# New instruction orders, earlier mask and x loads, and GpSimd splits from partition 0 in an LSH attention with a routed expert layer

## The chip, the cores and the metric

The kernel runs on one core of one Trainium2 chip, in one launch. The metric is the device time of that core in microseconds (us). Five engines work side by side, each through its own instruction queue in program order: TensorE (PE in the profile, its weight loads PEld), VectorE (DVE), ScalarE (ACT), GpSimd (POOL) and SyncE (SP, which here only issues DMAs).

## The reference

Inputs are q, k, v of shape (4, 8, 768, 64) in float32, a projection of 64x6, and the gate and two weight matrices of 8 experts (512x1024 and 1024x512). Attention is masked by hash buckets: a query sees only the keys whose six sign bits agree with its own. The output goes through an expert layer in which each token goes to one expert.

```python
q_bits = (np.einsum('bhsd,dk->bhsk', q, proj) > 0)      # likewise k_bits; bucket = the 6 bits as a number
mask = q_bucket[:, :, :, None] == k_bucket[:, :, None, :]
scores = np.where(mask, scale * np.matmul(q, k.transpose(0, 1, 3, 2)), -1e9)
attn = softmax(scores);  x = np.matmul(attn, v)          # rows of x: 3072 tokens x 512
expert_idx = np.argmax(x @ w_gate, axis=1)
y = np.maximum(x @ w1[e], 0.0) @ w2[e]                   # for the tokens of expert e
out = gate_w[:, None] * y
```

## The kernel before

**Pairs and passes.** The 32 heads are worked as 16 pairs (4 batches of 4 pairs). The loop at line 1076 makes one pass for each pair and runs through a written list of short tokens: HEAD in pass 0, PLAN in passes 1 to 14, LAST in pass 15. `step` (line 986) turns a token into instructions. A token with "-" behind it belongs to the pair before (one "-" for each pair back), so a pass g mixes the scores of pair g with the end of pairs g-1 and g-2 and the preparation of pair g+1. Every engine executes its share of the tokens in the order of the list. The lists are thus the order of the work on all queues.

**The tokens of a pass.** A pair has 12 score units (128 queries of one head by 768 keys).
- S: four matmuls of a unit (lines 291 and 293) into one of three PSUM tiles named s. R: VectorE takes the row's extreme and copies to SBUF (line 301), which frees the PSUM tile. X: ScalarE's exponential (line 307).
- The probabilities are then transposed, for one half of the units by TensorE (T, line 321, evacuated by E, lines 369 and 371, through two PSUM tiles named t), for the other half by VectorE in 32x32 blocks (D, line 343) into one SBUF tile `ZT`. Behind the sixth D of a pair, SyncE issues 16 DMAs (line 349) that carry the blocks to their places in `pt`. `ZT` has one buffer (the room named w2, and w0 for the last two pairs), so the first D of a pair waits until the 16 DMAs of the pair before have landed.
- V: probabilities times v (24 matmuls, line 381), O its evacuation (line 387). K and L: the rows of the pair with the gate's product (lines 401 and 411). M: the sums (line 391).
- I: SyncE's loads for pair g+2, `loads` (line 953): q and k of the pair for the hash (`load_pair`, line 82), q and k of each head (`load_x`, line 77, 768 KB each), v (`load_v`, line 87, which waits for the V of the pair before), and in the early passes the filling of the rows that no token takes (`fill`, line 148, 1.2 MB each, for the eight experts in turn).

**The preparation of the next pair.** A: ScalarE scales k (line 1039). P0 to P3 for one head and P4 to P7 for the other: GpSimd splits q and k into a high and a low part (`split`, lines 186 to 200) in a tile of four planes. Plane 2 and plane 3 get hash bits in 16 rows. G: TensorE's hash products (line 249), H: their signs on ScalarE (line 232), B: GpSimd weighs them and writes them to memory (lines 259 and 260). N: GpSimd issues two DMAs (line 264) that bring the bits into planes 2 and 3 of the two heads, once P1, P2, P5 and P6 are done and B's write has landed. In the code this is called a mask; the first S of the next pair waits for it.

**Routing.** When a batch of four pairs is done, its tokens are routed (`route`, line 421, a chain of small VectorE operations with a few matmuls in between, of which the tokens R and G of the next passes carry some steps each) and their rows are written to the expert's rows by GpSimd's indirect DMAs (`scatter`, line 475, in passes 7, 8, 11, 12, 14 and 15, one behind an R each). `route_step` (line 936) says behind which R of a pass: k counts the R tokens of the pass.

**The expert layer.** In LAST, GpSimd also prepares the first expert's weights (n and t, lines 898 and 904; `weights`, lines 655 and 656) in the rooms w0 to w3, and the first matmuls of the expert layer are put in (m, line 763). From then on the expert layer runs through all experts (lines 763, 800, 820).

**Last pair.** Its x is loaded at the start of pass 14 (line 1079), into the tiles named xd. The x of the other odd pairs goes into `room`, the room w3 (line 71).

## Time and profile before

| what | value |
|---|---|
| time, median of 3 runs (lowest to highest) | 754.92 us (747.46 to 757.76) |
| the profiled execution's own time | 753.52 us |
| its span in the profile | 751.7 us |
| TensorE busy | 707.0 us, 94% of the span |
| VectorE, ScalarE, GpSimd busy | 452.1, 428.3, 458.0 us |
| DMA, mean over the span | 195 GB/s |

The profile shows one execution. A row of its groups of instructions gives the line of the kernel, the engine, the operation, and out<-in by the names of the tiles; in a timeline, the start, the duration, the engine and line, and in brackets how long the engine had been idle before and what ended the wait. PEclk is the clock granted to TensorE, as a share of full speed. The pass borders used below are the starts of TensorE's first instruction of a pass.

### The profile page before, as it was taken

To read this page: it belongs to the slowest core of one execution; us is meant where nothing else is said; L and a number is where in the kernel's file an instruction comes from. 1 tells how busy PE (TensorE), PEld (TensorE's weight loads), DVE (VectorE), ACT (ScalarE), POOL (GpSimd) and SP (SyncE) were. 2 spreads that over 40 slices of the span, in tenths; PEclk is the share of its full clock that TensorE was granted. 3 is DMA by queue.
4 is the path that set the end of the run, shared out by engine and by line. 5 is a ranking of instruction groups with operands and counts; after the bars stand their busy time and mean duration, and the time that the engine had idled before them with its cause. 6 is when DMAs were issued, how large, how long until landed. Compare 5 with 4: busy or idle time off the path is not lost.

```text
span 751.7 us, 12370 instructions
## 1 busy us (share of the span) xinstructions
PE 707.0 (94%) x4219; PEld 578.0 (77%) x4219; DVE 452.1 (60%) x929; ACT 428.3 (57%) x864; POOL 458.0 (61%) x492
## 2 busy tenths in 40 slices
...
GB/s 314 214 265 229 279 265 308 295 150 283 294 206 242 231 243 276 241 271 150 171 228 174 117 96 83 254 152 169 170 130 164 142 132 185 191 131 189 125 10 38
DMA packets 68849, 146.69 MB, mean 195 GB/s; under 512 B 15811, under 2 KB 29507, under 8 KB 68720
## 3 DMA queue, kind: packets, MB, share of 16 engines
...
q10 hardware_dynamic: 144, 0.02, 0.0%
HBM read 89.35 MB, written 26.33 MB: 154 GB/s over the span
## 4 chain that ended last, share of the span: by engine, by line
PE 48%; DMA 13%; POOL 8%; issue 3%; DVE 2%; ACT 2%; SPq 1%; POOLq 0%; DVEq 0%; ACTq 0%
PE s L763 20%; PE s L800 10%; PE s L820 9%; DMA masks<-bits 4%; DMA w<-masks 3%; DMA sorted_rows<-xr,slot 2%; PE t L321 2%; PE t L381 2%; PE s L291 2%; PE s L293 2%; DMA qk<-masks 1%; SPq L349 1%; POOL w L197 1%; DMA sorted_rows<-sorted_rows 1%; POOL qk L197 1%
## 5 line engine op out<-in xcount | busy, mean ns | idle before, releaser
L301 DVE TENSOR_SCALAR_CACHE_REDUCE e<-s 128x768 f32<-128x768 f32 x192 | 178.8, 948 | 79.7 <-PE s L293 46.6
L307 ACT ACTIVATE e<-e,m 128x768 f32<-128x768 f32 x192 | 178.2, 931 | 10.6 <-DVE e L301 8.1
L659 POOL TENSOR_TENSOR w<-raw,w 128x512 fp32r<-128x512 f32 x112 | 144.8, 1316 | 36.2 <-ACT w L658 35.0
L381 PE MATMUL t<-pt,vt 128*64 128x384 f32 x768 | 129.5, 493 | 3.9 <-ACT pt L371 3.9
L763 PE MATMUL s<-xh,w 128*128 128x456 f32 (+6 forms) x672 | 126.8, 346 | 0.0
L371 ACT ACTIVATE pt<-t 128x512 f32<-128x512 f32 (+1 forms) x152 | 84.3, 584 | 72.1 <-PE t L321 69.6
L763 PEld LDWEIGHTS s<-xh,w 128*128 128x128 f32 x672 | 119.2, 188 | 3.1
L381 PEld LDWEIGHTS t<-pt,vt 128*64 128x64 f32 x768 | 54.2, 138 | 71.5 <-issue 64.2
L779 DVE SCALAR_TENSOR_TENSOR hh<-s,hh 128x256 fp32r<-128x256 f32 (+7 forms) x64 | 35.5, 555 | 107.1 <-ACT hh L777 100.3
L321 PE MATMUL t<-ident,e 128*128 128x128 f32 x648 | 95.3, 283 | 3.2 <-ACT e L307 2.1
L343 DVE STREAM_TRANSPOSE w<-e 128x768 f32<-128x768 f32 x84 | 77.5, 957 | 24.0 <-DMA pt<-w 13.9
L321 PEld LDWEIGHTS t<-ident,e 128*128 128x128 f32 x648 | 79.6, 146 | 12.7 <-ACT e L307 3.8
L777 ACT ACTIVATE hh<-s 128x256 fp32r<-128x256 f32 (+7 forms) x64 | 31.4, 490 | 90.8 <-PE s L763 90.8
L800 PE MATMUL s<-hh,w 128*128 128x456 f32 (+3 forms) x384 | 74.9, 355 | 0.0
L800 PEld LDWEIGHTS s<-hh,w 128*128 128x128 f32 x384 | 71.1, 188 | 2.7
L291 PE MATMUL s<-qk 80*128 80x384 f32 x192 | 57.6, 383 | 13.1 <-DMA qk<-masks 11.9
L291 PE MATMUL s<-w 80*128 80x384 f32 x192 | 56.2, 374 | 13.8 <-DMA w<-masks 13.8
L658 ACT ACTIVATE w<-raw 128x512 fp32r<-128x512 f32 x112 | 66.3, 622 | 0.6 <-DMA raw<-in_w1p_dram 0.6
...
L820 PE MATMUL s<-w,hh 128*128 128x512 f32 (+1 forms) x240 | 56.4, 394 | 0.0
L820 PEld LDWEIGHTS s<-w,hh 128*128 128x128 f32 (+1 forms) x240 | 44.6, 187 | 10.5
L293 PE MATMUL s<-qk 128*128 128x384 f32 x192 | 52.1, 355 | 0.0
...
## 6 DMA issues: line engine op xcount, KB each, us to landing
...
```

The lines of the kernel that those rows point to most:

```text
L291: nc.tensor.matmul(p[:, a, :HALF], k[0:80, 2, c], k[0:80, 3, n], start=i >= 4, stop=i < 4)
L293: nc.tensor.matmul(p[:, a, :HALF], k[:, 0, c], k[:, 1, n], start=i < 4, stop=i >= 4)
L301: nc.vector.tensor_scalar(e, SC.pop(i)[:, :, :HALF], CEIL, None, op0=OP.min, op1=OP.min, accum_out=m)
L307: nc.scalar.activation(e, e, AF.Exp, bias=m, scale=-1.0, accum_out=SM[g, hf][:, t, s:s + 1])
L321: nc.tensor.transpose(o[:, j, w], e[w][:, kt // 3, (kt % 3) * 128:(kt % 3) * 128 + 128], ident)
L343: nc.vector.transpose(z[:, :, c, w].rearrange("p g (k i) -> p g k i", i=32), e)
L371: nc.scalar.activation(o, x, AF.Copy)
L381: nc.tensor.matmul(p[s * 64:(s + 1) * 64, :HALF], VT[g][:, kt, s, :], PT[u][:, :, :, s, kt].rearrange("p a t i -> p t a i"), start=(kt == ...
L659: nc.gpsimd.tensor_tensor(w[:, 1, a], r, w[:, 0, a], op=OP.subtract)
L763: nc.tensor.matmul(p[:, :c], w[:, a, d, fs], x[:, b, d, :c], start=(k == 0), stop=(k == 11))
L800: nc.tensor.matmul(p[:, :c], w[:, a, f % 4, ms], h[b][:, f, :c], start=(k == 0), stop=(k == 23))
L820: nc.tensor.matmul(p[:pw], HH[n][b][:, f, i:i + pw], w[:, a, f % 4], start=(k == 0), stop=(k == 23))
```

## The change

- `split` k = 3 (P3, P7): the copy of q covers all 128 partitions, and the subtraction that makes the low part works on partitions 0 to 63 in place of 64 to 127 (it takes the high part from the tile's own plane 0 in place of plane 2). High and low halves of plane 0 change places; the product over both halves is the same sum.
- The last pair's x goes into `room` like that of other odd pairs and is loaded by token I of pass 13 in place of at the start of pass 14. Its split tiles move to the rooms w2 and w1, and the first expert's weight chunks to the rooms in the order of HOME.
- `fill` of experts 2 to 7: expert 2 in pass 0 behind token w, experts 3 to 7 in passes 1 to 5 (before: experts 2 to 7 in passes 1 to 6).
- `route_step`: the first seven steps of a batch's routing run behind R number 7 to 11 of the pass in portions of 2, 1, 2, 1 and 1 (before: one behind each of R number 2 to 8).
- New lists HEAD, PLAN and LAST with nearly the same tokens. In PLAN, G, H and B stand at the head of the pass, N stands ahead of V1 and V0 in place of behind them, the splits come in the order P5 P1 P0 P2 P4 P6 N P7 P3 (before P5 P7 P4 P6 P0 P1 P2 N P3).

```diff
@@ -72,7 +72,7 @@
 
     def load_x(h):
         g = h // 2
-        x = room[:, h % 2] if g % 2 and g < NG - 1 else wk.tile([128, 2 * S], F32, name="xd")
+        x = room[:, h % 2] if g % 2 else wk.tile([128, 2 * S], F32, name="xd")
         for c in ((S, 2 * S), (0, S)) if h < 2 else ((0, 2 * S),):
             nc.sync.dma_start(x[:, c[0]:c[1]], qk2[h][:, c[0]:c[1]])
         XD[h] = x
@@ -176,7 +176,7 @@
     def qk_tile(h):
         g = h // 2
         if g == NG - 1:
-            QK[h] = moe.tile([128, 4, S], F32R, name=f"w{2 + h % 2}")
+            QK[h] = moe.tile([128, 4, S], F32R, name=f"w{2 - h % 2}")
         elif g % 2 and g < NG - 1:
             QK[h] = moe.tile([128, 4, S], F32R, name=f"w{h % 2}")
         else:
@@ -196,8 +196,8 @@
         elif k == 2:
             nc.gpsimd.tensor_tensor(t[0:80, 3], x[0:80, S:], t[0:80, 1], op=OP.subtract)
         else:
-            nc.gpsimd.tensor_copy(t[0:64, 0], x[0:64, :S])
-            nc.gpsimd.tensor_tensor(t[64:128, 0], x[64:128, :S], t[64:128, 2], op=OP.subtract)
+            nc.gpsimd.tensor_copy(t[:, 0], x[:, :S])
+            nc.gpsimd.tensor_tensor(t[0:64, 0], x[0:64, :S], t[0:64, 0], op=OP.subtract)
 
     ENG = {"A": nc.scalar, "V": nc.vector, "P": nc.gpsimd}
 
@@ -626,6 +626,7 @@
 
 
     CH, RAW = {}, {}
+    HOME = "w0", "w3", "w2", "w1", "w4", "w5"
     P2 = {}
 
     def raw_load(c, a):
@@ -649,7 +650,7 @@
 
         if a == 0:
             s = c % 6
-            CH[c] = (moe if s < 4 else P2["p"]).tile([128, 2, 4, 512], F32R, name=f"w{s}")
+            CH[c] = (moe if s < 4 else P2["p"]).tile([128, 2, 4, 512], F32R, name=HOME[s])
         w, r = CH[c], RAW[c, a // 2][:, a % 2]
         if c < 4:
             nc.gpsimd.tensor_copy(w[:, 0, a], r)
@@ -890,7 +891,7 @@
             k = parts.pop(0)
             c, a = divmod(k, 4)
             if a == 0:
-                CH[c] = moe.tile([128, 2, 4, 512], F32R, name=f"w{c}")
+                CH[c] = moe.tile([128, 2, 4, 512], F32R, name=HOME[c])
             o, i = CH[c][:, 0, a], RAW[c, a // 2][:, a % 2]
             if x == "A":
                 nc.scalar.activation(o, i, AF.Copy)
@@ -909,26 +910,26 @@
     lows = []
 
     HEAD = """
-        k01A k00V j00V y01 q00A j01V p00A y00 l00V b03 b00 i02 f0 p01P b02 q01P b01 k11A i12 f1 k10A j11V y11 R0 j10V
-        l01P y10 q11P l11P q10A l10P S1 S8 p11P p10A b10 b13 b12 X0 s10 R1 X1 S2 G H w R8 X8 s12 R2 X2 S5 R5 X5 s01 S6
-        s00 S3 T01 s02 z0 S4 s11 z1 s13 b11 E01v s03 T00 E00a T02 R3 S7 E02v X3 T10 E10a R4 X4 T11 T12 E11v E12a R6 X6
-        R7 X7 T20 E20v S9 T21 E21v S10 T22 R9 E22a T30 E30a X9 T31 E31v T32 E32a R10 S11 R11 T41 E41a X10 T40 E40v T42
-        E42v
+        k01A k00V j00V y01 q00A j01V p00A y00 l00V b03 b00 i02 f0 p01P b02 q01P b01 k11A i12 f1 k10A j11V y11 R0 l01P
+        q10A p10A b13 y10 j10V b12 q11P b10 p11P S8 R8 S2 R2 G l10P S3 R3 l11P X0 H w S6 R6 S1 S4 X2 X3 T11 s11 s00
+        s01 s02 S5 b11 X6 X8 s10 s12 z1 z0 E11v s13 T10 E10v T12 R1 S9 X1 T01 R9 E12a E01v X9 T00 E00v S7 T02 E02a R7
+        R4 T41 E41a T40 T42 E40a E42v R5 S10 X7 T31 E31v T30 E30v S11 T32 E32v X4 X5 T20 E20a T21 M0 E21a T22 R11 X11
+        s03 E22v
     """.split()
 
     PLAN = """
-        K1-- R6- R10- X6- L0-- R11- T31- X10- E31a- X11- P5 S1 L1-- R1 S3 T30- E30a- T32- S5 E32a- T50- T51- R3 P7
-        E50a- S4 T52- E51a- R5 R4 S0 X3 S2 G A1 P4 E52a- S9 X4 X1 R2 H X5 S8 V1- M0- A0 X2 P6 B D3 O1- D1 R8 P0 D4 P1
-        V0- R0 R9 X8 X0 S7 X9 O0- D2 D0 T41 E41a I T40 S6 D5 S10 T42 P2 E40a R7 M1- X7 E42a N K0- P3 S11
+        R6- G L0-- X6- H P5 T30- S1 R11- T31- E30a- B R10- R1 K1-- X11- P1 S4 E31a- T32- L1-- S2 X10- M0- T50- R4
+        E32a- T51- E50a- S5 R2 M1- A0 T52- X4 E52a- P0 E51a- X2 A1 P2 P4 X1 R5 S3 S0 R3 S9 D4 S8 P6 X5 N V1- D2 X3 R9
+        O1- D5 V0- R0 R8 X9 D3 X0 S7 X8 I O0- T41 P7 E41a T40 D0 D1 R7 S6 T42 E40a S11 K0- E42a P3 X7 S10
     """.split()
 
     LAST = """
-        nP nP R6- X6- R10- X10- R11- T30- nP S3 tP L0-- E30v- S2 tP R2 X11- M1- T51- E51a- T50- E50a- X2 tP S0 T52-
-        E52a- R3 X3 R0 S7 K1-- L1-- S1 T31- E31v- X0 S5 T32- R1 E32a- X1 V1- O1- R5 X5 T01 E01v T00 E00a nP tP S4 T02
-        E02a T10 E10a R4 nP tP nP tP R7 S10 M0- T11 E11a nP tP X4 X7 S9 T12 R10 X10 E12v R9 X9 V0- O0- x2 g2 h2 S11
-        T20 E20a K0- L0- M0 nP tP S6 T21 E21a S8 T22 E22a R6 R11 X11 X6 V0 O0 T50 E50a T51 E51a T52 E52a R8 T30 E30a
-        T31 E31v T32 E32v X8 T40 E40a T41 E41a T42 E42a K0 L0 r0 r0 r0 M1 V1 r0 O1 K1 r0 r0 r0 L1 c0 K1- L1- r1 r1 r1
-        r1 r1 r1 r1 c1 x0 g0 h0 m6 u6 d6 m7 u7 d7 m4 u4 m3 u3 d4 d3 m2 u2 d2 m1 u1 d1 m0 u0 d0 m5 u5 d5
+        nP tP R6- X6- R11- L0-- K1-- L1-- R10- M0- X11- T31- M1-- E31a- T30- E30a- T32- S5 E32v- nP tP S4 X10- T50-
+        E50a- T51- E51a- R5 X5 R4 X4 S0 R0 X0 S3 T52- E52v- R3 X3 M1- S1 R1 X1 S6 V1- O1- T00 E00a S10 T20 E20a T21
+        E21v S2 T22 R2 R10 X10 E22v V0- O0- nP tP T01 T02 E01v E02v S8 X2 T11 E11a T10 E10a R6 X6 nP tP nP tP nP tP R8
+        X8 S11 K1- L1- M0 nP tP S9 K0- L0- S7 nP tP T12 E12a V0 R11 X11 R9 X9 O0 T41 E41a T40 T42 E40a E42a T51 E51a
+        R7 X7 K0 L0 r0 r0 T50 E50a T52 E52a T30 E30a r0 x0 T31 E31v T32 E32a x2 g2 r0 h2 M1 r0 r0 r0 c0 V1 O1 K1 L1 r1
+        r1 r1 r1 r1 r1 r1 c1 g0 h0 m2 u2 m3 u3 m4 d2 u4 m6 u6 d3 d4 d6 m7 u7 d7 m5 u5 d5 m0 u0 d0 m1 u1 d1
     """.split()
 
     SCAT = {}
@@ -936,10 +937,10 @@
     def route_step(g, k, since):
 
         b, q = divmod(g - NP, NP)
-        if 0 <= b < B - 1 and q == 1 and k == 2:
-            routes[b] = route(b, (0, 1))
-        if 0 <= b < B - 1 and q == 1 and k != "G" and 2 <= k <= 8:
-            go(routes[b], 1)
+        if 0 <= b < B - 1 and q == 1 and k != "G" and k >= 7:
+            if k == 7:
+                routes[b] = route(b, (0, 1))
+            go(routes[b], (2, 1, 2, 1, 1)[k - 7])
         if 0 <= b < B - 1 and q == 2:
             go(routes[b], 2 if k == "G" else 1 if since in (1, 2) else 0)
         if g in (7, 8, 11, 12) and k in (2, 5, 8) or g == 14 and since in (3, 4, 5) or g == 15 and k in (0, 1, 2):
@@ -954,7 +955,7 @@
 
         if g + 2 < NG:
             load_pair(g + 2)
-        if g + 2 < NG - 1:
+        if g + 2 < NG:
             load_x(2 * g + 4)
             load_x(2 * g + 5)
         if g + 1 < NG:
@@ -965,7 +966,7 @@
         g, r = divmod(c, 6)
         if 0 < g < NG - 1:
             return
-        if g + 2 < NG and r in (0, 2) and g + 2 != NG - 1:
+        if g + 2 < NG and r in (0, 2):
             load_x(2 * g + 4 + r // 2)
         if g + 1 < NG and r == 4:
             load_v(g + 1)
@@ -1008,8 +1009,8 @@
             trans(6 * n + int(x[0]), int(x[1]))
         elif op == "I":
             loads(n)
-            if 0 < n < 7:
-                fill(n + 1)
+            if 0 < n < 6:
+                fill(n + 2)
         elif op == "D" and n:
             blocks(12 * n + int(x))
         elif op == "E":
@@ -1075,9 +1076,6 @@
     last = [route(B - 1, (0,)), route(B - 1, (1,))]
     for g in range(NG):
         peaks, since = 0, 0
-        if g == NG - 2:
-            load_x(2 * g + 2)
-            load_x(2 * g + 3)
         for w in HEAD if g == 0 else LAST if g == NG - 1 else PLAN:
             if w == "G":
                 route_step(g, w, 0)
@@ -1085,6 +1083,8 @@
             step(g, w)
             if g == 0 and w in ("z0", "z1"):
                 fill(int(w[1]))
+            if g == 0 and w == "w":
+                fill(2)
             if w[0] == "R":
                 route_step(g, peaks, since)
                 if g == NG - 2 and 0 < since < 5:
```

## Rows read from the trace of the kernel before

**Rows 1.** The page's first part: busy time, share of the span, instructions.
```profile
PE 707.0 (94%) x4219; PEld 578.0 (77%) x4219; DVE 452.1 (60%) x929; ACT 428.3 (57%) x864; POOL 458.0 (61%) x492
```

**Rows 2.** Stretches: length, busy and (instructions) of PE PEld DVE ACT POOL, PEclk, DMA, GB/s.
```profile
52.20:79.40 27.20, 24.84 (x154) 18.66 (x154) 18.33 (x37) 18.97 (x39) 15.25 (x16) 0.94 0.85 248
...
104.10:127.10 23.00, 23.00 (x154) 17.15 (x153) 17.34 (x37) 18.70 (x39) 14.47 (x15) 1.00 0.95 295
...
150.50:182.30 31.80, 26.19 (x162) 19.97 (x161) 20.68 (x45) 19.39 (x39) 14.78 (x17) 0.89 0.68 205
...
356.60:386.10 29.50, 25.10 (x160) 17.76 (x159) 20.10 (x51) 19.27 (x41) 15.00 (x19) 0.94 0.58 176
386.10:443.90 57.80, 46.01 (x287) 32.31 (x287) 28.79 (x76) 27.33 (x54) 39.06 (x52) 0.90 0.49 152
443.90:751.70 307.80, 302.94 (x1655) 283.08 (x1655) 131.62 (x235) 116.46 (x233) 178.81 (x178) 0.99 0.50 141
```

**Rows 3.** Waits of TensorE: us in total, times, longest.
```profile
PE s L291 <- DMA w<-masks: 13.8, 6, 7.1
PE s L291 <- DMA qk<-masks: 11.9, 5, 5.5
```

**Rows 4.** Timeline of TensorE in passes 4, 6 and 15.
```profile
111.82 0.85 PE L249 MATMUL t<-xhe,pj 128*32 128x384 f32 x8
...
157.41 0.98 PE L291 MATMUL s<-qk 80*128 80x384 f32 x2 [5.46 <-DMA qk<-masks]
...
393.83 0.98 PE L291 MATMUL s<-w 80*128 80x384 f32 x2 [7.06 <-DMA w<-masks]
```

**Rows 5.** The stretch behind the mask wait of pass 6, columns as in rows 2.
```profile
157.40:163.00 5.60, 5.59 (x20) 5.50 (x21) 1.93 (x4) 1.20 (x2) 0.00 (x0) 0.50 0.84 219
```

**Rows 6.** The mask loads, line 264: what GpSimd waited for before them, and their landing.
```profile
  DMA masks<-bits: 31.4, 11
...
DMA to landing us min/median/max: 4.0/7.0/9.8
```

**Rows 7.** Timeline of GpSimd in pass 4.
```profile
111.79 0.82 POOL L193 CAST w<-w 128x768 fp32r<-128x768 f32 x1 [3.87 <-ACT w L1039]
...
115.42 0.63 POOL L260 DMA_DIRECT2D masks<-bits  x1 [0.30 <-POOL bits L259]
...
123.17 1.02 POOL L264 DMA_DIRECT2D w<-masks  x2 [3.63 <-DMA masks<-bits]
```

**Rows 8.** Line 200, the split that starts at partition 64: what GpSimd waited for.
```profile
  DMA sorted_rows<-xr,slot: 17.3, 5
```

**Rows 9.** Timeline of GpSimd in pass 7.
```profile
186.58 1.10 POOL L481 DMA_INDIRECT sorted_rows<-xr,slot  x1 [5.40 <-issue]
...
193.30 1.83 POOL L200 TENSOR_TENSOR qk<-xd,qk 64x768 fp32r<-64x768 f32 x1 [4.01 <-DMA sorted_rows<-xr,slot]
```

**Rows 10.** Timeline of SyncE's queue in pass 14: the last pair's x.
```profile
362.91 1.00 SPq L77 DMA_DIRECT2D xd<-in_qk_dram  x2
```

**Rows 11.** Timeline of GpSimd in passes 14 and 15.
```profile
369.89 0.82 POOL L195 CAST w<-xd 128x768 fp32r<-128x768 f32 x1 [16.53 <-DMA xd<-in_qk_dram]
370.65 0.82 POOL L199 CAST w<-xd 64x768 fp32r<-64x768 f32 x1
...
399.37 1.17 POOL L898 CAST w<-raw 128x512 fp32r<-128x512 f32 x2 [5.33 <-DMA pt<-w]
...
435.03 1.31 POOL L656 TENSOR_TENSOR w<-raw,w 128x512 fp32r<-128x512 f32 x1
```

**Rows 12.** Timeline of VectorE in passes 4 and 5.
```profile
116.36 1.84 DVE L343 STREAM_TRANSPOSE w<-e 128x768 f32<-128x768 f32 x2 [3.07 <-DMA pt<-w]
...
121.59 2.70 DVE L343 STREAM_TRANSPOSE w<-e 128x768 f32<-128x768 f32 x3
...
135.90 1.69 DVE L447 TENSOR_SCALAR oh<-rl 128x48 bf16<-128x48 f32 x1
...
139.85 1.84 DVE L343 STREAM_TRANSPOSE w<-e 128x768 f32<-128x768 f32 x2 [1.97 <-DMA pt<-w]
```

## The prediction, made before the changed kernel ran

> **What bounds the kernel now.** I read the page's busy times first, then the stretches by pass, the waits of TensorE, and the timelines around the longest of them. TensorE is busy for 94% of the span [rows 1], so a gain has to come from its gaps. The stretches say where they are: from 443.9 us on, in the expert layer, TensorE is busy 302.9 of 307.8 us [rows 2], and the change moves nothing there. Pass 4 is without a gap: 23.00 us long, TensorE busy 23.00 [rows 2]. That is the floor of a pass. Passes 2 to 14 run from 52.2 to 386.1 us [rows 2], 333.9 us for 13 passes, where 13 x 23.0 = 299.0 would do: 34.9 us too many. Pass 15 takes 57.8 us with TensorE busy 46.0 [rows 2].
>
> The waits name the main cause: the first S of a pass waits for the masks, 13.8 + 11.9 = 25.7 us in 11 waits [rows 3], up to 5.46 us in pass 6 and 7.06 us in pass 15 [rows 4]. A long wait costs twice. Behind that of pass 6 the granted clock is 0.50, the lower level of 1.2 GHz, for 5.6 us [rows 5], so that some 2.8 us more are lost (half of 5.6).
>
> Why the masks are late is in GpSimd's timeline. In pass 4 (start 104.1) the bits go out at 115.42, the mask loads at 123.17, after 3.63 us of waiting for the bits' landing [rows 7]; the landing of a mask load takes 4.0, 7.0, 9.8 us (least, median, most) [rows 6]. The first S of the next pass stands at 127.1 + 1.1. So the masks leave 5 us ahead of their use, which is less than the median. Everything that delays GpSimd comes on top, and three things do: the splits of line 200, which alone among the splits wait for the landing of the scattered rows, 17.3 us in 5 waits [rows 8]; the first scatter, 5.40 us in pass 7 [rows 9]; and the last pair's x, which SyncE issues only at 362.91, behind 16 block DMAs [rows 10], so that GpSimd sits idle for 16.53 us until 369.89 [rows 11] and pass 14 grows to 29.5 us.
>
> **The change part by part.**
>
> *Masks in mid pair, with G, H, B at the head.* Only the order changes. In pass 4 the bits go out 11.3 us into the pass; with G first (0.85 us [rows 4]), its sign and B right behind they go out at about 3, and land by 13 even if their write takes the 9.8 us of the longest landing [rows 6]. The splits that N needs are four short ones and two long ones: P1, P5, P0, P4 at 0.82 and P2, P6 at 1.83 (both from rows 9 and 11), 6.9 us; they are paced by A (ScalarE's scaling, which P0 waits for [rows 7]), and I estimate N at 14 to 15 us into the pass, where it stood at 19.1 (123.17 - 104.1). The first S stands one G and one T behind the border, at 23.0 + 0.85 + some 0.4 = 24.2 (the T an estimate), so the masks have 9 to 10 us in place of 5. With the median landing the wait is gone, with the longest 0 to 0.7 us is left.
>
> A rule of the Trainium skill speaks against this step: "DMA: Bandwidth & Descriptors", section "Issuing engines are not separate DMA queues", says that DMAs started from different engines run on the same 16 DMA engines and interleave. By it the masks, now issued in the stretch in which SyncE's loads of x run, would land at the late end of the range; it is taken up as rival 2.
>
> *Splits from partition 0.* The copy over 128 partitions takes 0.82 us, as that over 64 does [rows 11], and the subtraction keeps its 64 rows, so the work costs nothing. What goes is the wait of 17.3 us [rows 8], since no split that starts at partition 0 shows it. It is GpSimd time and counts for TensorE only through late masks; I book it there. If the wait stayed it would stand behind N now and delay only the next pass's P5: 0 to 1 us.
>
> *Empty rows one pass earlier.* The last fill is then issued a pass ahead of the first scatter, and the 5.40 us in front of it [rows 9] go. Again GpSimd time, booked with the masks of pass 8. Pass 0 takes one fill more on a DMA share that is high there; bounds for the first two passes -2 to +2 us, taken as 0.
>
> *The last pair's x.* It lands in pass 13; the 16.53 us of GpSimd go, and with them the excess of pass 14 (29.5 - 23.0 = 6.5). Next late is the tile in room w2: P1 and P0 of the last pair need it, and it holds the blocks of pair 13 until their 16 DMAs have landed, in pass 4 at 12.3 us into the pass (116.36 - 104.1) [rows 12]. So N of pass 14 comes at 18 to 19 and the first S of pass 15 may wait 0 to 3 us; I take 1.
>
> *The orders.* They put TensorE's tokens where R and X of the unit have had time, as before: the same 26 tokens of 23.0 us. What limits a pass next is a loop around the one tile `ZT`: six D with three R between (from 116.36 to 124.29), 16 DMAs, and the next first D at 139.85, waiting for their landing [rows 12]: 23.5 us, a little over TensorE's 23.0. The new list has the same six D and three R (D4 D2 R9 D5 R0 R8 D3 D0 D1), so the loop stays. I take 23.3 us for an ordinary pass, between the 23.0 of TensorE and the 23.5 of the loop.
>
> The routing steps are the one place where the new order looks worse: in passes 5, 9 and 13 four of the steps now fall between D's, the 1.69 us one [rows 12] and six of about 0.2 us, 2.9 us in all, that ran before the first D and in its wait of 1.97 us before. Bounds 0 (if the loop has that slack) and 2.9 a pass; I take 2.7, as D, R and the 16 DMAs leave none. In passes 6, 10 and 14 the last steps now stand at the head of the pass, where VectorE feeds the S tiles: 0 to 2, taken as 1 each.
>
> Sum for passes 2 to 14: 13 x 23.3 + 3 x 2.7 + 3 x 1 + 1 (the wait behind pass 14) + 1 for small new waits of T on E = 316.0, against 333.9: -17.9.
>
> *Pass 15.* Its mask wait of 7.06 us goes, and about 2.4 us at the lower clock behind it (393.8 to some 398.7). GpSimd doesn't get shorter: the first weights wait for the blocks of pair 14 until 399.37, 13.3 us into the pass, and its work then runs to 436.34 [rows 11]. It ends 50 us into the pass, as before, while TensorE's part shrinks to 48. The last scatter and the last weights so come 2 us behind TensorE's start of the expert layer in place of 7 ahead, and are first needed some 14 us into it. That cover is enough; if it weren't, the loss would be 0 to 7. Taken: -9.5.
>
> Total: -17.9 - 9.5 = -27.4 against the profiled execution's 753.52, so 726.1. That execution lies 1.4 us under the median of three (754.92) in runs from 747.46 to 757.76; I forecast 726 us.
>
> **The rivals.**
>
> 1. *VectorE's loop becomes the bound of every pass.* For it: the loop is already at 23.5 [rows 12], TensorE at 23.0, and D4 now stands ahead of R9, R0 and R8. Against it: six D and three R as before, and pass 4 ran at 23.0. If an ordinary pass takes 24.4, that is 13 x 1.1 = 14 us more: 740.
>
> 2. *The masks are still late; the change does not do what it says.* For it: the landing of up to 9.8 us [rows 6], and a DMA share of 0.95 in pass 4 [rows 2]. Against it: 4 us more room. Then the surplus of the passes stays, and only pass 14 (6.5 us less the wait of 1) gains: about 748. The rule of the Trainium skill above would bring this about; the landings of rows 6, from loads issued beside the block DMAs of SyncE, show only that the range is wide.
>
> 3. *Slower: the first D blocks the S tiles.* D4 stands in VectorE's queue ahead of R9, whose PSUM tile S7 needs 18 us into the pass. If the block DMAs land later than that, TensorE waits one to one, in each of 13 passes. They landed at 12.3 in pass 4, so it decides from 6 us later on. Landing at 21.4 costs 3.4 us a pass, 13 x 3.4 = 44 over my sum: 770. For it: the DMA share of 0.95, and the mask and x traffic that moves closer to the blocks. Against it: the same bytes per pass.
>
> 4. *Nothing new is late.* All passes at 23.0: 753.5 - 34.9 - 9.5 = 709.
>
> **How the numbers follow.** A measurement of this kernel can tell about 2% (15 us) from no change. My forecast (719 to 733) gets 0.5, rival 1 0.17, rival 2 0.12, rival 3 0.07, rival 4 0.12, and 0.02 is for none of them. Faster by over 2%, below 739.8: forecast, rival 4, half of rival 1 and a little of the rest, 0.74. Within 2%: half of rival 1 and most of rival 2, 0.19. Slower: rival 3, 0.07. The range goes from rival 4 (709) to 746, with rival 1 inside and rivals 2 and 3 outside.
>
> **What would show it right or wrong.** Right: TensorE's waits on masks at line 291 under 5 us in all; mask loads issued 14 to 15 us into a pass; no wait of line 200's successor on scattered rows; pass 14 at 23 to 25 us; no stretch at 0.50 behind a pass border; passes 5, 9 and 13 the longest, at about 26; start of the expert layer near 416. Wrong: ordinary passes over 24 with VectorE's first D waiting (rival 1), line 291 still waiting for masks (rival 2), S7 waiting for R9 (rival 3), or passes 5, 9 and 13 at 23.

## The result and the profile after

The changed kernel takes 726.43 us (median of 4 runs, 725.1 to 729.24) against 752.79 us of the kernel before on the same chip (4 runs, 747.46 to 757.76): ratio 0.9656, 95% interval 0.9579 to 0.9733. The forecast was 726.0. Medians here hold all runs of a kernel; ratios and intervals leave disturbed runs out, and the one profile of the last pair's x alone (below) is of such a run. The profiled execution took 726.39 us, with a span of 724.5 us.

The first part of the page of the changed kernel answers to [rows 1]: TensorE is busy 695.3 us in place of 707.0, with the same number of matmuls, so part of the gain is clock.

```profile
PE 695.3 (96%) x4219; PEld 567.4 (78%) x4219; DVE 453.3 (63%) x931; ACT 428.5 (59%) x862; POOL 458.1 (63%) x492
```

The stretches of the changed kernel, columns as in [rows 2]: pass 4 (an ordinary one), passes 5, 9 and 13 (routing), passes 14 and 15, the expert layer.

```profile
97.60:120.40 22.80, 22.80 (x153) 16.90 (x152) 17.95 (x37) 18.80 (x39) 14.42 (x14) 1.00 0.98 283
120.40:150.30 29.90, 25.96 (x160) 19.66 (x159) 21.08 (x47) 19.79 (x41) 14.40 (x14) 0.89 0.91 266
...
220.80:245.60 24.80, 23.38 (x163) 17.18 (x163) 22.30 (x46) 19.06 (x40) 14.44 (x14) 1.00 0.74 219
315.80:342.50 26.70, 23.39 (x164) 17.20 (x166) 22.64 (x46) 19.50 (x41) 14.44 (x14) 1.00 0.77 212
342.50:366.40 23.90, 23.57 (x153) 16.93 (x154) 20.94 (x52) 18.56 (x37) 15.08 (x19) 1.00 0.75 205
366.40:417.00 50.60, 43.19 (x288) 30.11 (x287) 29.84 (x77) 26.78 (x55) 37.02 (x47) 0.98 0.47 139
417.00:724.50 307.50, 302.24 (x1655) 282.22 (x1655) 131.99 (x235) 116.56 (x233) 179.93 (x182) 0.99 0.50 143
```

Passes 2 to 14 now run from 50.7 to 366.4, 315.7 us in place of 333.9: -18.2. Pass 15 gives -7.2, the head -1.5, the expert layer -0.3; together the -27.2 between the spans. Pass 14 fell from 29.5 to 23.9. Pass 6, with its mask wait and the lower clock 31.8 us long before, is at 22.9.

The waits of TensorE, columns as in [rows 3]. No row of it names masks any more. The longest are now those of the transposes T.

```profile
PE t L321 <- ACT e L307: 11.5, 8, 3.7
PE t L452 <- DVE ohs L447: 3.6, 1, 3.6
PE t L452 <- DVE pt L369: 1.7, 1, 1.7
PE s L764 <- DVE xhe L747: 1.4, 1, 1.4
```

The mask loads of line 264 answer to [rows 6]: they land as late as before, but leave 13.2 to 13.8 us into passes 2 to 13 (pass 5: 133.71 - 120.4 = 13.3) and 19.4 us into pass 14, and nobody waits for them. Line 200, where GpSimd had waited 17.3 us [rows 8], has no wait at all.

```profile
DMA to landing us min/median/max: 3.0/7.0/9.0
```

Most of what is left ahead of pass 15 stands at one place, T41 behind S7. It needs X8, which needs R8, which VectorE executes between its D's. TensorE's timeline in pass 5, and the stretch behind it:

```profile
142.95 1.97 PE L321 MATMUL t<-ident,e 128*128 128x128 f32 x8 [3.67 <-ACT e L307]
```

```profile
142.95:150.30 7.35, 7.08 (x37) 6.74 (x37) 3.58 (x8) 4.08 (x9) 0.83 (x1) 0.63 0.83 237
```

The wait of 3.67 us is paid twice here too: the granted clock behind it is 0.63 over 7.35 us, that is, mostly the lower level of 1.2 GHz. That is not so every time. In pass 13 TensorE waits 3.00 us at the same place, and its granted clock stays at 1.00, as the row of that pass shows.

VectorE's first D waits for the landing of the blocks in nearly every pass (its waits in the changed kernel):

```profile
DVE w L343 <- DMA pt<-w: 32.0, 11, 4.8
```

Whether that reaches TensorE is a matter of when the first D starts. In passes 4, 10 and 2 it starts 10.8, 11.8 and 12.0 us into the pass, and they take 22.9 us; in passes 12, 11, 3 and 8 it starts at 12.7, 12.8, 13.1 and 13.8, and they take 23.6, 23.7, 24.0 and 24.6. So an ordinary pass has slack until about 12 us and pays every microsecond behind that.

### The profile page after: what moved, and what is told of

It reads as the page before. It is cut to its first block, busy times and chain, and to the rows that moved or that the text cites. A ratio compares the mean times of both kernels' runs of the same rounds, so it can differ in the third digit from the quotient of the medians.

```text
span 724.5 us, 12349 instructions
## 1 busy us (share of the span) xinstructions
PE 695.3 (96%) x4219; PEld 567.4 (78%) x4219; DVE 453.3 (63%) x931; ACT 428.5 (59%) x862; POOL 458.1 (63%) x492
## 4 chain that ended last, share of the span: by engine, by line
PE 57%; SPq 14%; DVE 12%; issue 9%; DMA 5%; ACT 1%; POOL 1%; DVEq 0%; POOLq 0%; ACTq 0%
PE s L764 18%; SPq L349 14%; PE s L801 10%; PE s L821 8%; PE t L381 7%; DVE w L343 4%; PE t L321 4%; DMA pt<-w 4%; DVE e L301 3%; PE s L291 3%; PE s L293 3%; DMA sorted_rows<-sorted_rows 1%; PE t L401 1%; PE s L830 1%; POOL w L660 1%
## 5 line engine op out<-in xcount | busy, mean ns | idle before, releaser
L301 DVE TENSOR_SCALAR_CACHE_REDUCE e<-s 128x768 f32<-128x768 f32 x192 | 177.2, 946 | 26.6 <-PE t L321 13.5
L381 PE MATMUL t<-pt,vt 128*64 128x384 f32 x768 | 127.8, 488 | 0.0
L321 PE MATMUL t<-ident,e 128*128 128x128 f32 x648 | 95.1, 279 | 12.8 <-ACT e L307 11.5
L321 PEld LDWEIGHTS t<-ident,e 128*128 128x128 f32 x648 | 76.1, 142 | 32.2 <-ACT e L307 21.2
L291 PE MATMUL s<-qk 80*128 80x384 f32 x192 | 55.5, 372 | 1.3 <-DVE e L301 1.3
L821 PEld LDWEIGHTS s<-w,hh 128*128 128x128 f32 (+1 forms) x240 | 44.6, 187 | 10.5
L293 PE MATMUL s<-w 128*128 128x384 f32 x192 | 50.1, 342 | 0.0
```

The lines of the kernel that those rows point to most:

```text
L291: nc.tensor.matmul(p[:, a, :HALF], k[0:80, 2, c], k[0:80, 3, n], start=i >= 4, stop=i < 4)
L301: nc.vector.tensor_scalar(e, SC.pop(i)[:, :, :HALF], CEIL, None, op0=OP.min, op1=OP.min, accum_out=m)
L321: nc.tensor.transpose(o[:, j, w], e[w][:, kt // 3, (kt % 3) * 128:(kt % 3) * 128 + 128], ident)
L381: nc.tensor.matmul(p[s * 64:(s + 1) * 64, :HALF], VT[g][:, kt, s, :], PT[u][:, :, :, s, kt].rearrange("p a t i -> p t a i"), start=(kt == ...
L821: nc.tensor.matmul(p[:pw], HH[n][b][:, f, i:i + pw], w[:, a, f % 4], start=(k == 0), stop=(k == 23))
```

## The experiments

My theory was that the masks were the main cause, that the loop around `ZT` comes next, and that the routing steps cost what they take from VectorE. The runs came in four groups, each on a chip of its own; the kernel before had medians of 749.65, 754.53, 752.72 and 756.16 us in them. Differences of 2 or 3 us between groups thus rest on the profiles, and each of these shows one execution. How far a pass length can be trusted is seen in the run with the last x late: its edit reaches nothing before pass 13, yet its ordinary passes sum to 162.4 in place of 164.6 us. Likewise the run with the fill behind leaves pass 13 as it is, and that pass takes 29.3 in place of 26.7. TensorE's wait in it is 3.0 us in both; what differs is the granted clock (0.88 and 1.00). For the routing passes the waits are therefore the better measure. The table has the times, the pass lengths and those waits (us; lengths from the starts of TensorE's first instruction of a pass; "ordinary" is the sum of passes 2, 3, 4, 7, 8, 11 and 12; the last column is TensorE's idle time in passes 5, 9 and 13):

| kernel | median | passes 2-14 | ordinary | pass 5 | 9 | 13 | 14 | waits 5 / 9 / 13 |
|---|---|---|---|---|---|---|---|---|
| before | 752.8 | 333.9 | 176.0 | 23.4 | 24.1 | 25.2 | 29.5 | 0.2 / 0.9 / 2.0 |
| changed | 726.4 | 315.7 | 164.6 | 29.9 | 24.8 | 26.7 | 23.9 | 3.7 / 1.1 / 3.0 |
| masks alone | 738.7 | 325.3 | 167.3 | 26.0 | 26.1 | 27.7 | 29.8 | 2.2 / 1.9 / 2.3 |
| splits from partition 64 | 727.0 | 317.4 | 162.8 | 29.0 | 27.6 | 28.4 | 24.0 | 3.4 / 3.4 / 3.1 |
| steps early | 723.0 | 315.0 | 163.7 | 25.5 | 27.1 | 27.1 | 23.9 | 1.5 / 1.5 / 1.5 |
| steps spread | 725.5 | 316.2 | 163.4 | 27.1 | 27.0 | 27.0 | 23.9 | 1.7 / 1.7 / 1.7 |
| four DMAs more | 742.1 | 330.6 | 173.5 | 30.0 | 29.0 | 28.3 | 23.9 | 3.7 / 3.7 / 3.0 |
| fill behind | 723.6 | 313.7 | 160.3 | 29.5 | 24.8 | 29.3 | 23.9 | 3.0 / 1.1 / 3.0 |
| no low part | 720.2 | 310.8 | 162.0 | 28.4 | 23.6 | 27.1 | 23.9 | 2.9 / 0.0 / 1.8 |
| last x late | 729.6 | 316.4 | 162.4 | 28.8 | 24.8 | 28.3 | 26.3 | 3.7 / 1.1 / 3.0 |
| fill behind, R8 first | 728.1 | 314.1 | 161.8 | 29.3 | 26.6 | 26.6 | 23.9 | 2.9 / 2.9 / 2.9 |
| fill behind, fewer steps | 719.4 | 310.5 | 160.3 | 29.7 | 25.4 | 25.3 | 23.9 | 3.0 / 1.4 / 1.4 |
| the last, placed anew | 716.1 | 305.7 | 164.5 | 24.4 | 23.5 | 23.5 | 24.0 | 0.4 / 0.0 / 0.0 |

### Parts of the change by themselves

**Masks alone.** The kernel before, with PLAN changed in nothing but the places of G, H, B, A, the splits and N.

```diff
-        K1-- R6- R10- X6- L0-- R11- T31- X10- E31a- X11- P5 S1 L1-- R1 S3 T30- E30a- T32- S5 E32a- T50- T51- R3 P7
-        E50a- S4 T52- E51a- R5 R4 S0 X3 S2 G A1 P4 E52a- S9 X4 X1 R2 H X5 S8 V1- M0- A0 X2 P6 B D3 O1- D1 R8 P0 D4 P1
-        V0- R0 R9 X8 X0 S7 X9 O0- D2 D0 T41 E41a I T40 S6 D5 S10 T42 P2 E40a R7 M1- X7 E42a N K0- P3 S11
+        R6- G L0-- X6- H K1-- R10- R11- P5 T31- X10- E31a- B X11- S1 P1 L1-- R1 S3 T30- E30a- T32- S5 E32a- T50- T51- R3
+        E50a- S4 T52- A0 E51a- R5 R4 S0 P0 X3 S2 A1 E52a- P2 P4 S9 X4 X1 R2 P6 X5 N S8 V1- M0- X2 D3 O1- D1 R8 P7 D4 V0- R0 R9 X8 X0
+        S7 X9 O0- D2 D0 T41 E41a I T40 S6 D5 S10 T42 E40a P3 R7 M1- X7 E42a K0- S11
```

> The kernel before, with one edit: in PLAN the tokens G, H and B go to the head of the pass, A and the splits are put in the order P5 P1 P0 P2 P4 P6 N P7 P3 and N stands ahead of V1 (R6, K1, L0 move by a place or two to make room); HEAD, LAST, fills, splits and the last pair's x stay. If late masks were the cause of the long passes, TensorE's 25.7 us of waits on masks shrink to the one of pass 15 (about 7) and passes 2 to 13, 304.4 us before, come to 12 x 23.5 = 282: 22 us less, ratio 0.97. If it is the whole new order that carries the gain, this alone gives under 8 us, ratio above 0.99.

738.74 us (738.16 to 740.89), ratio 0.9861 (0.979 to 0.9933): about 11 us, less than half of the whole and between the two expectations. The wait for masks is all but gone, as in the changed kernel, but the S tiles now wait for VectorE's R. TensorE's waits in this run:

```profile
PE s L291 <- DVE e L301: 15.4, 16, 3.3
...
PE s L291 <- DMA w<-masks: 2.2, 2, 1.6
```

Of the 15.4 us, 6.4 are in passes 5, 9 and 13, 3.3 in pass 14, and 0.4 in each ordinary pass. What the masks alone leave to the whole change is 12.8 us by the spans (737.3 and 724.5), and most of it lies elsewhere: 4.3 us ahead of pass 2, 5.9 in pass 14, where x is still late, and 3.7 in passes 2 to 13 (295.5 and 291.8, from 304.4 before); behind pass 14 it is 1.1 the other way. So in passes 2 to 13 the masks gave 8.9 of 12.6 us. The new order of S and R, which stood at nothing in my sum, was not run by itself; net, it can be seen in no more than the 3.7.

**The last pair's x alone**, in the kernel before (lines 75, 957, 968, 1079 and the rooms, as in the change).

> The kernel before, with the last pair's x alone: loaded by token I of pass 13 into the room of the other odd pairs, its split tiles in rooms w2 and w1, the weight chunks in the order of HOME; orders, fills and splits as before. If the late x is what lengthened pass 14 and delayed the masks of pass 15, GpSimd's wait of 16.5 us goes, pass 14 falls from 29.5 to about 24 and the mask wait of 7.1 us with its stretch at the lower clock to 0 to 3 us: 8 to 14 us less, ratio 0.981 to 0.990. If GpSimd's late work in pass 15 sets the end there, 5 to 7 us less, ratio 0.991 to 0.993.

The median is 750.23 us (737.87 to 765.25), ratio 0.9889 (0.9786 to 0.9992): a gain of some 1%, with a wide interval. Pass 14 is at 25.3 us in place of 29.5. The other half of the expectation failed: in this profile TensorE still waits 6.7 us for masks at the head of pass 15, where I had expected 0 to 3, so the late x alone was not the cause of that wait.

**The last pair's x late**, in the changed kernel.

```diff
-        if g + 2 < NG:
+        if g + 2 < NG - 1:
             load_x(2 * g + 4)
...
+        if g == NG - 2:
+            load_x(2 * g + 2)
+            load_x(2 * g + 3)
```

> The changed kernel with the last pair's x loaded at the start of pass 14, as before the change (its tile and the rooms stay as changed). Mine (the loads then stand behind 16 block DMAs in SyncE's queue, so x lands some 13 us into pass 14; ScalarE's scaling A of that x stands in its queue at some 7 us, ahead of the X of pass 14): pass 14 grows from 23.9 by 5 to 6.5 us, pass 15 waits 0 to 3 us for masks, the time is 732 to 735 us. Rival (with the new order the late x is covered, since nothing of TensorE's pass 14 needs it): less than 1.5 us, 726 to 728 us.

729.63 us (728.34 to 732.93), 3.2 us more than the changed kernel and between the two expectations. ScalarE waits where I had named it. Timelines of ScalarE, GpSimd and TensorE in pass 14 (start 341.4):

```profile
351.21 0.84 ACT L1040 ACTIVATE w<-w 128x768 f32<-128x768 f32 x1 [3.33 <-DMA w<-in_qk_dram]
```
```profile
353.32 0.83 POOL L195 CAST w<-w 128x768 fp32r<-128x768 f32 x1 [20.45 <-DMA w<-in_qk_dram]
```
```profile
354.03 0.62 PE L291 MATMUL s<-qk 80*128 80x384 f32 x2 [2.58 <-DVE e L301]
```

ScalarE waits 3.33 us for x, in front of the X's; TensorE loses 2.4 us in pass 14 (26.3 against 23.9). GpSimd's idle 20 us cost little beyond that: one wait for masks of 1.0 us in pass 15. In the new order the late x costs pass 14 2.4 us; with the whole change pass 14 fell by 5.6.

**Splits from partition 64**, in the changed kernel.

```diff
-            nc.gpsimd.tensor_copy(t[:, 0], x[:, :S])
-            nc.gpsimd.tensor_tensor(t[0:64, 0], x[0:64, :S], t[0:64, 0], op=OP.subtract)
+            nc.gpsimd.tensor_copy(t[0:64, 0], x[0:64, :S])
+            nc.gpsimd.tensor_tensor(t[64:128, 0], x[64:128, :S], t[64:128, 2], op=OP.subtract)
```

> The changed kernel, with the splits of line 200 back on partitions 64 to 127 (copy on 64 partitions, subtraction from plane 2). My theory: the waits for scattered rows return on GpSimd (10 to 20 us in passes 7, 8, 11, 12 and 14), but P7 and P3 now stand behind the mask loads, so TensorE hardly sees them: 0 to 2 us more, ratio to the kernel before 0.966 to 0.969. Rival: they push the next pass's first splits and with them the masks, 5 to 10 us more, ratio 0.973 to 0.98.

726.96 us (725.52 to 730.99). In the waits of line 200 the landing of the scattered rows is back with 16.3 us in 3 waits, and the time is the same. With N ahead of P7 and P3 the masks no longer hang on them; TensorE waits for line 200 twice, 2.2 us together, in pass 9, and nowhere in the changed kernel. Why that split waits for the scatter was not tried.

### The loop and the fill

**Four DMAs more** behind the 16 block DMAs.

```diff
+            for a in range(4):
+                nc.sync.dma_start(extra[a], z[32 * a:32 * a + 32, a].rearrange("p c w x -> p (c w x)"))
             del ZT[g]
```

> The changed kernel with four more DMAs behind the 16 block DMAs of each pair (each reads a quarter of ZT and writes it to a scratch in memory that nobody reads), so that ZT comes free later by four issues of some 0.7 us. Mine (an ordinary pass is set by the loop around ZT, 23.5 against 23.0 us of TensorE): the first D of a pass starts some 3 us later, passes 2 to 14 grow by 2 to 3 us each, 26 to 39 us in all, about 757 us. Rival (TensorE sets the pass, the loop has slack, and the excess over 23.0 has other causes): VectorE waits longer for the landing, but passes 2 to 14 grow by less than 0.5 us each, 0 to 6 us in all, 726 to 732 us.

742.06 us (740.13 to 745.04): +15.6, between the two. The waits of VectorE's first D, and of T:

```profile
DVE w L344 <- DMA extra_blocks<-w: 43.3, 12, 5.9
```
```profile
PE t L322 <- ACT e L308: 20.6, 11, 3.7
```

The four issues take 2.0 us of SyncE's queue in most passes, behind 10 to 13.5 us for the 16 block DMAs. In the seven ordinary passes VectorE's first D starts 1.3 us later than in the changed kernel (on average 13.7 in place of 12.4 us into the pass), and these passes are 1.3 us longer (173.5 in place of 164.6). This fits the slack until about 12 us: pass 4, with its first D at 13.1, takes 23.9 here, and passes 6 and 10, with 10.8, stay at 22.9. Neither "no slack" nor "hidden" is right.

**Fill behind**: the fill of passes 1 to 5 is issued behind the block DMAs.

```diff
             if 0 < n < 6:
-                fill(n + 2)
+                C["late"] = n + 2
...
+            if "late" in C:
+                fill(C.pop("late"))
             del ZT[g]
```

> The changed kernel, but the fill of empty rows of passes 1 to 5 is issued behind the 16 block DMAs of the pair before it in SyncE's queue, in place of ahead of them. Mine (pass 5 is 29.9 us because a fill of 1.2 MB stands ahead of the block DMAs, whose landing holds back the first D by 3.48 us, and then the routing steps): pass 5 falls by 2 to 4 us, pass 3 by 1 us (24.0 to 23), the sum 3 to 5 us less, about 722 us. Rival (pass 5 is long from its routing steps alone, the landing is hidden as in passes 9 and 13): pass 5 stays within 1 us of 29.9, the time within 2 us of 726.

723.58 us (721.89 to 725.76), by the medians 2.9 us less than the changed kernel. The first D of pass 3 starts at 10.5 in place of 13.1 us into the pass, that of pass 5 at 11.6 in place of 13.4, and all seven ordinary passes are at 22.9. Of these, pass 3 alone (1.1 us) can be put down to the fill: passes 8, 11 and 12 have none, and with the fill ahead they were at 22.9 to 23.0 too in the runs with the last x late and with no low part. But pass 5 stays at 29.5: the first D is in time, and the pass is long all the same. There my explanation fell, and the rival's held: its routing steps make it long even without the late landing. VectorE's first D in pass 5 of this run, behind a wait of 1.60 us (3.48 us in the changed kernel):

```profile
131.16 1.84 DVE L343 STREAM_TRANSPOSE w<-e 128x768 f32<-128x768 f32 x2 [1.60 <-DMA pt<-w]
```

### The routing steps

**Steps early**: the first seven steps behind R number 2, 4, 4, 5, 6, 6 and 7, ahead of the first D.

```diff
-        if 0 <= b < B - 1 and q == 1 and k != "G" and k >= 7:
-            if k == 7:
+        if 0 <= b < B - 1 and q == 1 and k != "G":
+            if k == 2:
                 routes[b] = route(b, (0, 1))
-            go(routes[b], (2, 1, 2, 1, 1)[k - 7])
+            go(routes.get(b, iter(())), {2: 1, 4: 2, 5: 1, 6: 2, 7: 1}.get(k, 0))
```

> The changed kernel, with the seven routing steps of passes 5, 9 and 13 behind R number 2, 4, 4, 5, 6, 6 and 7 of the pass, so that all stand ahead of the pass's first D, where VectorE waits for the block DMAs. My theory: the steps between the D's are what makes these passes 29.9, 24.8 and 26.7 us long (12.4 us over 3 x 23.0), the part over 23.0 goes down to 0.5 to 1.5 a pass and the time by 8 to 11 us, to about 717, ratio 0.953. Rival: those passes are long because their first D waits for the DMAs anyway; then the time moves by less than 3 us.

722.99 us (719.82 to 729.15). The gap has moved from T41 to S9 and S8, which wait for an R, and has become shorter, 1.5 us in each of the three passes. Pass 5 fell to 25.5 us; passes 9 and 13 are no shorter than in the changed kernel, as their granted clock is 0.94 in place of 1.00. That the place between the D's is the whole cost was wrong.

**Steps spread**: the same with `{2: 1, 4: 1, 5: 1, 6: 1, 7: 1, 10: 1, 11: 1}`.

> The changed kernel with the first seven routing steps one behind each of R number 2, 4, 5, 6, 7, 10 and 11 of passes 5, 9 and 13 (in the changed kernel 2, 1, 2, 1, 1 behind R number 7 to 11). Theory 1 (a step costs what it takes from VectorE only where two or more stand ahead of the R that the next S waits for; GpSimd's subtractions hold the short operations up only in the second half of a pass): passes 5, 9 and 13 at 23.5 to 25, no gap ahead of S9 and S8, 5 to 9 us less, about 718 us. Theory 2 (VectorE has no slack in a routing pass, so the steps cost their sum of some 3 us a pass wherever they stand): passes 9 and 13 at 25 to 27 as in the changed kernel and in the run with all steps early, 722 to 726 us.

725.52 us (723.65 to 731.74); passes 5, 9 and 13 at 27.0 to 27.1, with a gap of 1.7 us ahead of S8 in each and a granted clock of 0.94. This looked like the second theory, but its trace shows another thing. VectorE and GpSimd in pass 9 of this run:

```profile
228.90 1.68 DVE L440 TENSOR_SCALAR rl<-rl 128x48 f32<-128x48 f32 x1
```
```profile
228.70 1.83 POOL L197 TENSOR_TENSOR qk<-xd,qk 80x768 fp32r<-80x768 f32 x1
```

The comparison of line 440 takes 0.18 us in pass 9 of the changed kernel. Here it takes 1.68, and ends at 230.58, 0.05 us behind GpSimd's subtraction beside it (228.70 + 1.83 = 230.53). S8 waits for the R behind it. In the changed kernel the same shows at other steps (VectorE and GpSimd in its pass 9):

```profile
235.87 0.18 DVE L440 TENSOR_SCALAR rl<-rl 128x48 f32<-128x48 f32 x1
236.08 1.81 DVE L441 TENSOR_TENSOR rl<-rl,desc 128x48 f32<-128x48 f32 x1
...
238.16 0.50 DVE L444 TENSOR_TENSOR rl<-desc,rf 128x48 f32<-128x48 f32 x1
...
239.46 1.07 DVE L447 TENSOR_SCALAR oh<-rl 128x48 bf16<-128x48 f32 x1
```
```profile
236.01 1.82 POOL L200 TENSOR_TENSOR qk<-xd,qk 64x768 fp32r<-64x768 f32 x1
237.78 0.81 POOL L199 CAST qk<-xd 128x768 fp32r<-128x768 f32 x1
238.67 1.81 POOL L200 TENSOR_TENSOR qk<-xd,qk 64x768 fp32r<-64x768 f32 x1
```

Each long one ends within 0.1 us of the end of the GpSimd operation beside it: 237.89 and 237.83, 238.66 and 238.59, 240.53 and 240.48. So the duration is mostly a wait, which the profile counts as busy time of VectorE.

**No low part**: the changed kernel without the subtraction of line 200 for the pairs prepared in passes 5, 9 and 13.

```diff
-            nc.gpsimd.tensor_tensor(t[0:64, 0], x[0:64, :S], t[0:64, 0], op=OP.subtract)
+            if h // 2 not in (6, 10, 14):
+                nc.gpsimd.tensor_tensor(t[0:64, 0], x[0:64, :S], t[0:64, 0], op=OP.subtract)
```

> The changed kernel, but without GpSimd's subtraction of line 200 for the pairs prepared in passes 5, 9 and 13 (the low part of q is left out there: those half planes keep the copy). Theory 1 (the routing operations of VectorE with two inputs, 0.2 us alone, last until GpSimd's subtraction beside them ends): those of line 441 and 447 fall from 1.81 and 1.07 us in pass 9 to 0.2 to 0.9 (a copy of 0.83 us may still stand beside one), VectorE gains 1 to 3 us in each of the three passes, and they get shorter by 0.5 to 3 us, 2 to 6 us in all: about 722 us. Theory 2 (these durations belong to the operation and its place): the durations stay, the time within 1.5 us of 726.

720.18 us (717.95 to 721.68), by the medians 6.2 us less than the changed kernel. In pass 9 of this run (lines one higher from 200 on) the product of line 442 is at 0.21 us, and what is left long stands beside the two copies, which end at 234.21:

```profile
233.33 0.92 DVE L441 TENSOR_SCALAR rl<-rl 128x48 f32<-128x48 f32 x1
234.28 0.21 DVE L442 TENSOR_TENSOR rl<-rl,desc 128x48 f32<-128x48 f32 x1
```
```profile
232.59 1.62 POOL L199 CAST qk<-xd 128x768 fp32r<-128x768 f32 x2
```

TensorE's waits in passes 5, 9 and 13 fall by 0.8, 1.1 and 1.2 us. Passes 5 and 9 are 1.5 and 1.2 us shorter; pass 13 is not, at a granted clock of 0.94 in place of 1.00, and there one step of 2.25 us ran until the second copy had ended. The first theory holds for the durations. Of the 6.2 us only the 2.3 of these three passes can be put down to the edit: the 2.6 in ordinary passes, which it leaves as they were, are of the size seen with the last x late (2.2).

**Fewer steps**: the fill behind, and the routing with three operations of the sensitive kind between the D's in place of five.

```diff
-        nc.vector.tensor_tensor(lg, lg, bc(mx), op=OP.subtract)
...
-        nc.vector.tensor_scalar(eq, lg, 0.0, None, op0=OP.is_equal)
+        nc.vector.tensor_tensor(eq, lg, bc(mx), op=OP.is_equal)
...
-        nc.vector.tensor_tensor(eq, dsc, bc(fi), op=OP.subtract)
...
-        nc.vector.tensor_scalar(oh[:, :nt], eq, 0.0, None, op0=OP.is_equal)
+        nc.vector.tensor_tensor(oh[:, :nt], dsc, bc(fi), op=OP.is_equal)
...
+        nc.vector.tensor_tensor(lg, lg, bc(mx), op=OP.subtract)
...
-            go(routes[b], (2, 1, 2, 1, 1)[k - 7])
+            go(routes[b], (2, 1, 2, 0, 2)[k - 7])
```

> The kernel of the run with the fill behind the block DMAs, with the same routing written in fewer VectorE operations: the maximum is found by a comparison with the row's maximum in place of subtraction and comparison (the subtraction for the exponential comes later, behind R number 11), and the one-hot of the expert by one comparison in place of subtraction and comparison. Of the short operations that stand between the D's of passes 5, 9 and 13 (lines 437, 440, 441, 444, 447) three are left. Theory 1 (each of them can last until GpSimd's operation beside it ends): passes 5, 9 and 13, which were 29.5, 24.8 and 29.3 us with the fill behind, get 1 to 3 us shorter each, 3 to 7 us in all, about 718 us. Theory 2 (they cost their own 0.2 us): 0.4 to 0.8 us a pass, 722 us.

719.38 us (718.5 to 721.77), by the medians 4.2 less than with the fill behind alone. The gain is in pass 13 (29.3 to 25.3) alone: its wait falls from 3.0 to 1.4 us, and its granted clock is 1.00 in place of 0.88; in passes 5 and 9 two of the three that are left still stood beside lines 199 and 200 (the product 0.86 and 1.75 us, the one-hot 1.62 and 0.49).

**R8 first**: with the fill behind, units 9, 8, 0 in this order.

```diff
-        E32a- T51- E50a- S5 R2 M1- A0 T52- X4 E52a- P0 E51a- X2 A1 P2 P4 X1 R5 S3 S0 R3 S9 D4 S8 P6 X5 N V1- D2 X3 R9
-        O1- D5 V0- R0 R8 X9 D3 X0 S7 X8 I O0- T41 P7 E41a T40 D0 D1 R7 S6 T42 E40a S11 K0- E42a P3 X7 S10
+        E32a- T51- E50a- S5 R2 M1- A0 T52- X4 E52a- P0 E51a- X2 A1 P2 P4 X1 R5 S3 S9 R3 S8 D4 S0 P6 X5 N V1- D2 X3 R9
+        O1- D5 V0- R8 R0 X9 X8 D3 X0 S7 I O0- T41 P7 E41a T40 D0 D1 R7 S6 T42 E40a S11 K0- E42a P3 X7 S10
```

> The kernel of the run with the fill behind the block DMAs, with the units 9, 8, 0 worked in this order in place of 0, 9, 8 (S3 S9 S8 S0, and R9 R8 R0), so that R8, whose exponential T41 needs, comes one R earlier, and S7, which needed the PSUM tile of unit 0, needs that of unit 9. Mine (T41 waits for X8 behind R8, and VectorE is late there in the routing passes): the waits of T41 fall by 0.9 us in each of passes 5, 9 and 13 (29.5, 24.8 and 29.3 us with the fill behind), some 2.5 us in all, about 721 us, and ordinary passes stay at 22.9. Rival (VectorE's last D's and R7 are late all the same, and the wait moves behind T41): the sum within 1 us of 723.6.

728.11 us (725.17 to 729.94), no gain. T41 no longer waits; T40 does, 2.9 us in each of the three passes. TensorE in pass 9, and ScalarE just before:

```profile
241.12 0.65 PE L321 MATMUL t<-ident,e 128*128 128x128 f32 x4 [2.92 <-ACT ot L389]
```
```profile
239.67 0.93 ACT L307 ACTIVATE e<-e,m 128x768 f32<-128x768 f32 x1 [2.65 <-DVE oh L449]
```

X0 now waits for the delayed R0 at the head of ScalarE's queue, and O0, which frees the PSUM tile of T40, stands behind it. A wait that is moved along takes what is queued behind it.

**Placed anew**: fewer steps, put by what GpSimd does there.

```diff
-            go(routes[b], (2, 1, 2, 0, 2)[k - 7])
+            go(routes[b], (4, 1, 0, 0, 2)[k - 7])
```

> The kernel of the run with fewer routing operations and the fill behind the block DMAs, with the steps placed by what stands beside them: the sums, the maximum, the comparison and the product all behind R number 7, ahead of the first D, where VectorE waits 0.8 to 2.4 us for the landing of the blocks and GpSimd is idle or copies; the second maximum and the one-hot behind R number 8, before GpSimd's subtractions of line 200; the rest behind R number 11. Theory 1 (the steps cost a pass only what they wait beside GpSimd): no short operation longer than 0.9 us, the D's of passes 5, 9 and 13 follow without the stretches of 2 to 5 us, passes 9 and 13 at 22.9 to 23.7 us (25.4 and 25.3 before this edit), pass 5 at 24 to 26 (29.7), the time 709 to 713 us. Theory 2 (they cost their own time in a full VectorE wherever they stand): passes 9 and 13 at 24.5 to 25.5, pass 5 at 28 to 30, the time 717 to 720 us.

716.09 us (715.12 to 718.49, 6 runs), ratio 0.9591 (0.9544 to 0.9638): its slowest run is below the fastest of either kernel. (The ratio of the run with fewer steps is 0.9557, but against another group's runs of the kernel before; passes 2 to 14 are 305.7 us here and 310.5 there.) The stretches of passes 5, 7, 9 and 13, and VectorE's steps in pass 9:

```profile
119.50:143.90 24.40, 23.71 (x160) 17.16 (x159) 19.57 (x46) 19.43 (x41) 14.40 (x14) 1.00 1.03 291
166.90:192.50 25.60, 23.31 (x153) 17.10 (x152) 17.78 (x37) 18.95 (x39) 18.72 (x22) 1.00 0.98 278
216.80:240.30 23.50, 23.21 (x160) 17.27 (x159) 19.56 (x46) 19.64 (x41) 14.46 (x14) 1.00 0.92 256
309.10:332.60 23.50, 23.19 (x164) 17.27 (x164) 19.57 (x45) 19.58 (x41) 14.45 (x14) 1.00 0.86 249
```
```profile
227.01 0.21 DVE L439 TENSOR_TENSOR rl<-rl,rf 128x48 f32<-128x48 f32 x1
227.25 0.21 DVE L442 TENSOR_TENSOR rl<-rl,desc 128x48 f32<-128x48 f32 x1
...
230.47 0.21 DVE L445 TENSOR_TENSOR oh<-desc,rf 128x48 bf16<-128x48 f32 x1
```

Every short operation of these three passes is at 0.2 to 0.3 us, and the routing passes are where the first theory put them, at 24.4, 23.5 and 23.5. The same steps in the same VectorE, in other places, cost 0.6 to 1.5 us a pass over 22.9 in place of the 2.4 to 6.8 of the run with fewer steps, and TensorE's waits there fall from 3.0, 1.4 and 1.4 us to 0.4, 0 and 0. The new places also lie where VectorE waits for the blocks. That alone is not the reason: with the steps early all seven stood ahead of the first D, and the waits were 1.5 us a pass. The time came out 3 us above the expectation; in the profile passes 7 and 8 (25.6 and 24.3) are the long ones: their first D waits for the blocks until 14.75 and 13.5 us, so the loop shows again.

## Why the prediction was right, and where not

**The cause and its main step: right.** The masks held TensorE; N leaves at 13.2 to 13.8 us (forecast 14 to 15) and in pass 14 at 19.4 (forecast 18 to 19), the landing is as before, line 291 waits for masks no more. Rival 2 fell: the landings went from 4.0/7.0/9.8 to 3.0/7.0/9.0. The rule of the Trainium skill that spoke for it ("DMA: Bandwidth & Descriptors", section "Issuing engines are not separate DMA queues": queues of different engines interleave on the same 16 DMA engines) did not show as later landings in this trace. By themselves early masks give 11 us, 8.9 of the 12.6 in passes 2 to 13. One thing was missing in the step: once the masks were there, the old order made S wait for R, and what the new order of S and R gave back, at most 3.7 us net, stood at nothing.

**Ordinary passes: right mechanism, small error.** Forecast 23.3, measured 23.5 (164.6 over 7; 23.1 and 23.2 in the runs with no low part and with the last x late, which leave these passes as they are). A loop of 23.5 beside TensorE's 23.0, without slack, was too simple: the loop has slack until the first D at 12 us, and what passes it is paid in full. Rival 1 is half true, in the passes with a late landing. Rival 3 had the right kind of mechanism (first D late), but the wait shows at T41, and from 12 us on, not at S7 from 18 on.

**Routing passes: wrong in size and cause.** Booked 2.7 each, 8.1; measured 6.9 + 1.8 + 3.7 = 12.4 over 23.0, of which TensorE's waits are 3.7, 1.1 and 3.0, and the lower clock of pass 5 some 2.6 (busy 25.96 us there, 23.38 in pass 9). The step that failed is "the 1.69 us one and six of about 0.2 us, 2.9 us in all": the 1.69 us of [rows 12] are no cost of that operation. GpSimd's timeline of the kernel before has a subtraction beside it that ends at 137.54:

```profile
135.70 1.84 POOL L197 TENSOR_TENSOR qk<-xd,qk 80x768 fp32r<-80x768 f32 x1
```

The operation ends at 135.90 + 1.69 = 137.59. Moved, it and its neighbours waited beside other ones. That the waits sum to 7.8, near the 8.1, is luck. That passes 5, 9 and 13 would be the longest was right.

**Passes 6, 10 and 14: wrong.** I booked 1 us each for the last steps at the head of the pass; passes 6 and 10 are at 22.9, so that cost is nothing, and the wait behind pass 14 (1 us) did not come either. Pass 14's 23.9 is within its forecast of 23 to 25.

**Fill: bound in the wrong place.** The 5.40 us in front of the first scatter are gone, as forecast. For the cost I looked at the first two passes (0, measured -1.5). It came in passes 3 and 5, where the fill stands ahead of the block DMAs: their first D starts 2.6 and 1.8 us later than in the run with the fill behind. In pass lengths that is 1.1 and 0.4 us; the 2.9 between the medians are not shown to be the fill's.

**The last pair's x: right in direction.** Pass 14 fell by 5.6 (forecast 5.5 with the wait taken off); by itself in the new order it is worth 3.2, of which 2.4 are in pass 14 and 1.0 is a wait for masks in pass 15.

**Splits from partition 0: right.** The wait is gone and worth next to nothing by now, as the 0 to 1 us booked for the case that it stayed had said: put back, it leaves the time as it is and costs TensorE 2.2 us of waits in one pass.

**Pass 15: -7.2 for -9.5.** The wait for masks (7.1) and the lower clock behind it went about as forecast: TensorE is busy 43.2 us in place of 46.0. But the end of the pass is the last batch's routing, for which TensorE has less left to do: its waits at line 452 are 1.7 + 3.6 us, where before there was one of 2.8 (the 1.4 at line 764 stands behind the border of the pass). I had weighed only GpSimd there.

So the match to 0.1% is partly luck: in passes 2 to 14, 4.9 us too little (1.5 ordinary, 3.4 routing) stand against 5.2 too much (3.2 in passes 6, 10 and 14, two waits of 1 us); outside them 2.3 too little in pass 15 stand against 1.8 too much in the head and the expert layer. And the run with the last x late, with the same code in passes 2 to 12, takes 3.4 us less for them (261.7 and 265.1).
